# The first four token tiles: centred before the transpose, scaled at the eviction

## Chip, cores and metric

The kernel runs on one core of a Trainium2 chip. A core has five engines that run side by side and meet only at semaphores: TensorE (PE; its weight loads are shown as PEld), VectorE (DVE), ScalarE (ACT), GpSimd (POOL) and SyncE (SP), which here issues every DMA. The metric is the device time of one execution in microseconds (us), median of the runs. All matrix operands are bf16, all sums f32.

## What is computed

There are 2048 tokens of width 512, and four layers that alternate two blocks A, B, A, B with the same weights: `x = x + A(layernorm(x))`, then `x = x + B(layernorm(x))`. The layer norm has no gain and no bias. Block B is `relu(x @ w1) @ w2` with an inner width of 1376. Block A is linear attention with 32 heads of width 16:

```
q, k, v = split(x @ wqkv)                 # each 2048 x 512
phi(t) = where(t > 0, t + 1, exp(t)) + 1e-6
kv  = sum over tokens of phi(k) v^T       # 16 x 16 for each head
z   = sum over tokens of phi(k)
o   = (phi(q) @ kv) / (phi(q) . z + 1e-6)
out = o @ wo
```

## The kernel before

**Tiles.** The tokens are 16 tiles of 128, or 4 chunks of 4 tiles. In SBUF `xin` holds the input, `xres` the f32 residual, `xn` the normalised rows, `Tb` their transposes, `big` the results of the projections. PSUM has 8 banks of 128x512 f32.

**Who sets the order.** Every operation is recorded with a name, its engine, what it reads and writes and an assumed cost. `_list_schedule` then makes one fixed order for each engine from those costs. `HINTS` shifts the rank of single operations, and `SEQS` fixes the first operations of an engine. On the chip every engine runs its list strictly in that order and waits on semaphores where the data demand it. Because one helper issues all matrix products, the profile gives them one line, L558; the names below are those of the recorded operations, with the layer or tile number at the end.

**Layer 0, where the change lies.** SP first issues the loads: tile 0 of x, tiles 1 to 3, the K part of `wqkv` in two halves (`ld_wk0`, `ld_wk1`), the next x chunk, the Q part (`ld_wq`), the other x chunks, the V part, `wo`, and then `w1` and `w2` for block B (L413 to L417). Meanwhile PE runs 11 matrix products on zeros (`warm`).

For tiles 0 to 2 DVE computes mean and variance (`bnst`, `bnag`) and adds epsilon (`veps_`), POOL raises that to the power -1/2 (`rstd_`), and DVE writes the normalised row to `xn` (`norm`, L814). ACT makes the sums for tile 3. PE then transposes a tile as four 128x128 blocks (`trp`, L523), and ACT or DVE copies the result from PSUM to `Tb` (`trev`, L527 and L528). Tiles 4 to 7 go the same way, with 1/sqrt by a logarithm and an exponential on ACT (`lnv`, `rstd`, L463 and L465). Tiles 8 to 15 are transposed by DMA (`tr2_0`, `tr2_1`, `tr3_0`, L506).

The K projection (`kproj`, four products of 512 columns) takes a tile of `Tb` as the stationary side, so that its result has tokens on the partitions. The Q projection (`qproj t_j`) takes a 128-column piece of the weights as the stationary side and four tiles of `Tb` as the moving one, so that its result has features on the partitions. `phi_evac` turns each projection into phi: ACT writes t + 1 + 1e-6 (`_lin`, L541) and exp(t) (`_exp`, L543) from PSUM, DVE clips the exponential (`_em`, L545) and takes the maximum of both (`_phi`, L551). A PSUM bank is free again when both have read it.

The products `g` (phi(k) with `xn`, for sum phi(k) x^T) are spread among the projections. `den` makes the denominators, 1/den is spread over partitions by 16 DMAs (`spread`), DVE multiplies it into phi(q) (`pqs`), and `fin` gives the output of block A, which DVE adds to x (`resid`).

Of the kernel before, what the change touches and what calls it, by code (L numbers as in the profile page):

```python
# [47 lines left out]
HINTS = {"0.fin8_0": -99, "0.g0_1_3": 10, "0.g1_1_1": 30, "0.g1_2_1": -496, "0.g1_2_2": -77, "0.k4_em": -180, "0.k5_em": -110,  # L48
         "0.pqs3_3": 37, "0.q0_0_em": 80, "0.q0_2_em": -70, "0.q0_2_phi": 30, "0.q0_3_em": 33, "0.q3_2_lin": 177, "0.q3_3_lin":
         30, "0.resid8": -373, "0.spread1_3": -17, "2.fin13_0": 200, "2.g0_0_0": 80, "2.norm0": -160, "2.q3_3_lin": 3,  # L50
         "2.qproj3_1": 10, "2.qproj3_2": -80, "2.spread0_0": 3, "2.spread0_3": -230, "2.spread1_0": 30, "2.spread1_2": 57,
         "2.var1": 610, "3.ffo10": 284, "3.h3_3_0": 83}

SEQS = {
    "dve": ["bnst0", "bnag0", "veps_0", "bnst1", "bnag1", "norm0", "veps_1", "bnst2", "trev0b", "bnag2", "veps_2", "norm1", "norm3",
            "norm2", "trev2"],
    "act": ["mean_3", "sq_3", "trev0a", "lnv_3", "rstd_3", "trev1", "trev3", "k0_lin", "k0_exp"],
    "pool": ["rstd_0", "nm2_3", "var_3", "veps_3", "rstd_1", "rstd_2"],
    "pe": ["trp0a", "trp0b", "kproj0a", "trp1", "kproj0b", "trp3", "kproj1", "trp2", "kproj3", "qproj0_0", "kproj2"],
}  # L60

# [208 lines left out]
def build_kernel(nc, A_x, A_wqkv, A_wo, B_w1, B_w2, out, n_layers_pairs=2, K_STT=0, Q_STT=0, A_PE_CHUNKS=0, windows=None,  # L270
                 WARM=11, SPLIT0=True, TAIL_SPLIT=True, LAST_HALVES=True, FIRST_PE_CHUNKS=2,
# [13 lines left out]
    EPS = 1e-5  # L285
# [5 lines left out]
    with es:  # L291
# [4 lines left out]
        xres = sb("xres", [128, NT, 512], F32)  # L296
        wqkv = sb("wqkv", [128, 4, 3 * D], BF16)
# [20 lines left out]
        NSCR = 12  # L318
        escr = sb("escr", [128, NSCR, 512], BF16)
# [86 lines left out]
        for t in range(2, NCH):  # L406
            ld_x(t)
        dma(lambda e: e.dma_start(wqkv[:, :, 2 * D:3 * D], wq_v[:, :, 2 * D:3 * D]), [], [("wv0",)], 1500.0, "ld_wv")
        dma(lambda e: e.dma_start(wvl[:], A_wqkv[D - 1:D, 2 * D:3 * D].broadcast_to([128, D])), [], [("wvl",)], 400.0, "ld_wvl")
        dma(lambda e: e.dma_start(wo[:], A_wo.rearrange("(c p) n -> p c n", p=128)), [], [("wo",)], 1500.0, "ld_wo")  # L410
        nfull = NFC - 1 if FLAST < 128 else NFC

        dma(lambda e: e.dma_start(w1[:], B_w1.rearrange("(c p) n -> p c n", p=128)), [], [("w1",)], 4000.0, "ld_w1")  # L413
        dma(lambda e: e.dma_start(w2[:, 0:nfull, :], B_w2[0:nfull * 128, :].rearrange("(c p) n -> p c n", p=128)),
            [], [("w2a",)], 3800.0, "ld_w2a")
        if FLAST < 128:
            dma(lambda e: e.dma_start(w2[0:FLAST, NFC - 1, :], B_w2[nfull * 128:DFF, :]), [], [("w2b",)], 600.0, "ld_w2b")  # L417
# [8 lines left out]
        if WARM > 0:  # L426
            wt = alloc_bank()

            def _warm(e):
                last = None  # L430
                for k in range(WARM):
                    last = e.matmul(psv[:, wt, :], wrm[:, 0:128], wrm[:, :], start=True, stop=True)
                return last
            g.add(PE, _warm, [("wrm",)], [("ps", wt)], 10 * 427.0 + (WARM - 10) * 216.0, name="warm")
# [23 lines left out]
        def ln_part_first(lo, hi):  # L458
            sl = slice(lo, hi)
            tl = range(lo, hi)  # L460
            g.add(DVE, lambda e: e.tensor_scalar(veps[:, sl], mv[:, sl, 1], 0.0, EPS, ALU.max, ALU.add),
                  [("var", i) for i in tl], [("veps1", i) for i in tl], C_DVE_SMALL, name="veps%d" % lo)
            g.add(ACT, lambda e: e.activation(var[:, sl], veps[:, sl], ACTF.Ln), [("veps1", i) for i in tl], [("lnv", lo)],  # L463
                  C_ACT_TINY, name="lnv%d" % lo)
            g.add(ACT, lambda e: e.activation(rstd[:, sl], var[:, sl], ACTF.Exp, scale=-0.5), [("lnv", lo)],  # L465
                  [("rstd", i) for i in tl], C_ACT_TINY, name="rstd%d" % lo)
# [70 lines left out]
        def phi_evac(b, dst_ap, dst_key, name, stt):  # L537
            s = scr_state["e"]
            scr_state["e"] = (s + 1) % NSCR
            if not stt:  # L540
                g.add(ACT, lambda e: e.activation(dst_ap, psv[:, b, :], ACTF.Identity, bias=1.0 + 1e-6, scale=1.0),  # L541
                      [("ps", b)], [dst_key], C_ACT_PSUM, name=name + "_lin")
            g.add(ACT, lambda e: e.activation(escr[:, s, :], psv[:, b, :], ACTF.Exp),  # L543
                  [("ps", b)], [("escr", s)], C_ACT_EXP, name=name + "_exp")
            g.add(DVE, lambda e: e.tensor_scalar(escr[:, s, :], escr[:, s, :], 1.0, 1e-6, ALU.min, ALU.add),  # L545
                  [("escr", s)], [("escr", s)], C_DVE_BF4X, name=name + "_em")
            if stt:
                g.add(DVE, lambda e: e.scalar_tensor_tensor(dst_ap, psv[:, b, :], 1.0 + 1e-6, escr[:, s, :], ALU.add, ALU.max),
                      [("ps", b), ("escr", s)], [dst_key], C_DVE_PSUM, name=name + "_phi")
            else:  # L550
                g.add(DVE, lambda e: e.tensor_tensor(dst_ap, dst_ap, escr[:, s, :], ALU.max),  # L551
                      [dst_key, ("escr", s)], [dst_key], 340.0, name=name + "_phi")
# [25 lines left out]
        def a_k(i):  # L578
# [5 lines left out]
            phi_evac(b, pk_tile(i), ("big", pk_unit(i)), "k%d" % i, stt=(i % 4) < K_STT)  # L584
# [64 lines left out]
        def a_q(t, js=(0, 1, 2, 3)):  # L649
            for j in js:  # L650
# [5 lines left out]
                phi_evac(b, unit_ap(u), ("big", u), "q%d_%d" % (t, j), stt=j < Q_STT)  # L656

        def a_den(t):
# [3 lines left out]
            mm_group(lambda: [(psv[32 * j:32 * j + 32, b, :], Zc[:, j, :], unit_ap(pq_unit(j, t)), True, True, False) for j in range(4)],  # L662
                     [("Zc",)] + [("big", pq_unit(j, t)) for j in range(4)], [("ps", b)], 400.0, "den%d" % t)
# [15 lines left out]
        def a_pqs(t):  # L679
            for j in range(4):  # L680
                u, r = pq_unit(j, t), rb_unit(t, j)
                g.add(DVE, lambda e, u=u, r=r: e.tensor_tensor(unit_ap(u), unit_ap(u), unit_ap(r), ALU.mult),
                      [("big", r), ("big", u)], [("big", u)], 340.0, name="pqs%d_%d" % (t, j))

        def a_fin_mm(i, b, js):
            t, il = i // 4, i % 4

            def mk():
                mms = []
                for j in js:  # L690
                    u = pq_unit(j, t)
                    mms.append((psv[:, b, :], big[:, u * 512 + 128 * il:u * 512 + 128 * il + 128], Mf[:, j, :], j == 0, j == 3, False))
                return mms
            mm_group(mk, [("big", pq_unit(j, t)) for j in js] + [("Mf", j) for j in js], [("ps", b)],
# [109 lines left out]
        def ln_own(i):  # L804
            mu = mv[:, i, 0:1] if i < 3 else mean[:, i:i + 1]
            if i == 3:
                g.add(ACT, lambda e: e.activation(var[:, i:i + 1], veps[:, i:i + 1], ACTF.Ln), [("veps1", i)], [("lnv1", i)],
                      C_ACT_TINY, name="lnv_%d" % i)
                g.add(ACT, lambda e: e.activation(rstd[:, i:i + 1], var[:, i:i + 1], ACTF.Exp, scale=-0.5), [("lnv1", i)],
                      [("rstd1", i)], C_ACT_TINY, name="rstd_%d" % i)  # L810
            else:
                g.add(POOL, lambda e: e.tensor_tensor(rstd[:, i:i + 1], veps[:, i:i + 1], nhalf[:, 0:1], ALU.pow),
                      [("veps1", i), ("nhalf",)], [("rstd1", i)], C_POOL_POW1, name="rstd_%d" % i)
            g.add(DVE, lambda e: e.tensor_scalar(xn[:, i, :], xin[:, i, :], mu, rstd[:, i:i + 1], ALU.subtract, ALU.mult),  # L814
                  [("xin", i), ("mean", i), ("rstd1", i)], [("xn", i)], C_DVE_NORM_BF, name="norm%d" % i)
            transpose_pe(i)

        def ln_first(t):
            if t == 0 and SPLIT0:
                for i in range(3):  # L820
                    ln_stats_first(i, [[], [("veps1", 0)], [("xn", 0), ("veps1", 1)]][i])
                    g.add(DVE, lambda e, i=i: e.tensor_scalar(veps[:, i:i + 1], mv[:, i, 1:2], 0.0, EPS, ALU.max, ALU.add),  # L822
                          [("var", i)], [("veps1", i)], C_DVE_TINY, name="veps_%d" % i)
                    ln_own(i)
# [8 lines left out]
                g.add(POOL, lambda e: e.tensor_scalar(veps[:, 3:4], var[:, 3:4], 0.0, EPS, ALU.max, ALU.add),  # L833
                      [("var", 3)], [("veps1", 3)], 150.0, name="veps_3")
                ln_own(3)
                ones_col(0)
# [272 lines left out]
```

## Time and profile before

| | |
|---|---|
| device time, median of 3 runs | 281.34 us (281.33 to 281.36) |
| span of the profiled execution, first to last instruction | 279.2 us |
| so outside that span | about 2.1 us |
| PE busy | 274.7 us, 98% |
| ACT busy | 174.4 us, 62% |
| DVE busy | 139.3 us, 50% |
| POOL busy | 43.4 us, 16% |
| granted TensorE clock | 1.000 |

The page gives one time of the profiled execution itself, its span. The times of the three runs are taken from outside and are 2.1 us longer; that part lies before the first and after the last instruction. Busy time of PE is not a measure of its speed, because the ends of its products are modelled; what tells whether PE lost time is the distance from start to start. Shares over the whole span hide the beginning, where the change lies: the windows and the timeline of the first 30 us have to be read for it.

### The profile page before, as it was taken

The numbers are of one execution on the slowest core, as the hardware profiler recorded it, in microseconds if no ns is written. First come the engines' busy times: TensorE is split into PE (matmuls) and PEld (weight loads), VectorE is DVE, ScalarE is ACT, GpSimd is POOL, SyncE is SP. The second block draws the span as 40 slices with busy tenths as digits, with TensorE's granted clock in tenths as the row PEclk, the third lists the DMA queues.
The fourth block names the chain that finished last, engine by engine and source line by source line (L and its number), as shares of the span: only waits on it lengthen the run. The fifth ranks groups of instructions, "written<-read, shape, count | busy, mean of one in ns | idle before, by whom it ended". The sixth has DMA issues, their size and how long they took to land.

```text
span 279.2 us, 4216 instructions
## 1 busy us (share of the span) xinstructions
PE 274.7 (98%) x1574; PEld 140.2 (50%) x1574; DVE 139.3 (50%) x379; ACT 174.4 (62%) x367; POOL 43.4 (16%) x120
## 2 busy tenths in 40 slices
PE   7999999999999999999999999999999999999996
PEld 2546556546544544544444455664654554454443
DVE  5999963899301362443363576279935300110222
ACT  5899978778773682677373799765884376226000
POOL 6000000046300160400040400003136100000000
PEclk9999999999999999999999999999999999999999
DMA  6999300833900053060003030084331641021012
GB/s 215 367 378 160 58 2 17 199 87 76 171 19 0 2 96 75 0 96 0 0 10 68 0 75 0 2 191 115 75 77 20 167 77 21 0 75 21 0 75 75
DMA packets 44276, 22.09 MB, mean 79 GB/s; under 512 B 34560, under 2 KB 42720, under 8 KB 44256
## 3 DMA queue, kind: packets, MB, share of 16 engines
q1 hardware_dynamic: 44256, 21.83, 32.9%
q8 instruction: 12, 0.20, 0.3%
q14 instruction: 8, 0.07, 0.1%
HBM read 7.14 MB, written 2.10 MB: 33 GB/s over the span
## 4 chain that ended last, share of the span: by engine, by line
PE 97%; DVE 1%; DMA 1%; issue 0%; DVEq 0%
PE ps L558 96%; DMA xin<-in_A_x_dram 1%; DVE bst L455 1%; PE ps L523 1%; DVE xn L814 0%; DVE mv L456 0%; DVE veps L822 0%; DVE xin L774 0%; DVE Tb L528 0%; DVEq L1037 0%
## 5 line engine op out<-in xcount | busy, mean ns | idle before, releaser
L558 PE MATMUL ps<-w,big 128*128 128x512 bf16 (+3 forms) x363 | 77.5, 373 | 0.0
L558 PE MATMUL ps<-Tb,w 128*128 128x512 bf16 (+1 forms) x352 | 70.9, 360 | 0.0
L754 ACT ACTIVATE big<-ps 128x512 bf16<-128x512 f32 x72 | 42.8, 596 | 24.7 <-PE ps L558 24.6
L558 PEld LDWEIGHTS ps<-w,big 128*128 128x128 bf16 (+1 forms) x363 | 35.0, 98 | 41.2 <-ACT big L754 0.3
L558 PEld LDWEIGHTS ps<-Tb,w 128*128 128x128 bf16 x352 | 33.9, 98 | 32.8
L575 ACT ACTIVATE sqscr<-xres 128x512 bf16<-128x512 f32 x48 | 29.9, 623 | 30.0 <-DVE xres L569 29.7
L541 ACT ACTIVATE big<-ps 128x512 bf16<-128x512 f32 x64 | 41.1, 646 | 6.0 <-PE ps L558 6.0
L569 DVE SCALAR_TENSOR_TENSOR xres<-ps,xres 128x512 f32<-128x512 f32 x32 | 21.2, 689 | 43.4 <-PE ps L558 43.4
L543 ACT ACTIVATE escr<-ps 128x512 bf16<-128x512 f32 x64 | 41.4, 655 | 1.3 <-PE ps L558 1.3
L566 DVE TENSOR_TENSOR xin<-ps,xres 128x512 bf16<-128x512 f32 x15 | 10.4, 691 | 49.7 <-PE ps L558 49.7
L558 PE MATMUL ps<-big,xn 128*128 128x256 bf16 (+1 forms) x224 | 31.0, 288 | 0.0
L558 PE MATMUL ps<-Tb,wqkv 128*128 128x512 bf16 x128 | 30.6, 379 | 0.0
L558 PE MATMUL ps<-wqkv,Tb 128*128 128x512 bf16 x128 | 30.1, 379 | 0.4 <-ACT Tb L527 0.4
L558 PE MATMUL ps<-Mf,big 128*128 128x512 bf16 x128 | 28.8, 379 | 0.0
L545 DVE TENSOR_SCALAR escr<-escr 128x512 bf16<-128x512 bf16 x64 | 18.3, 293 | 20.2 <-ACT escr L543 19.9
L551 DVE TENSOR_TENSOR big<-big,escr 128x512 bf16<-128x512 bf16 x64 | 26.5, 425 | 1.4
L558 PEld LDWEIGHTS ps<-big,xn 128*128 128x128 bf16 x224 | 21.5, 98 | 9.0 <-issue 0.8
L471 POOL TENSOR_SCALAR mean<-s 128x4 f32<-128x4 f32 x12 | 2.9, 245 | 123.9 <-DVE xres L569 123.9
L558 PEld LDWEIGHTS ps<-Mf,big 128*128 128x128 bf16 x128 | 12.3, 98 | 14.6 <-ACT Mf L645 0.5
L558 PEld LDWEIGHTS ps<-wqkv,Tb 128*128 128x128 bf16 x128 | 12.2, 98 | 14.3 <-ACT Tb L527 0.7
L558 PEld LDWEIGHTS ps<-Tb,wqkv 128*128 128x128 bf16 x128 | 12.4, 98 | 12.7 <-DVE Tb L528 0.3
L493 DVE TENSOR_SCALAR xn<-xres,mean,rstd 128x512 bf16<-128x512 f32 x23 | 14.8, 679 | 3.7 <-POOL nbias L483 3.5
(78 smaller groups left out, 188.2 us busy)
## 6 DMA issues: line engine op xcount, KB each, us to landing
big<-rdc SPq DMA_DIRECT2D x32, 128.0 KB, 2.6
xin<-in_A_x_dram SPq DMA_DIRECT2D x3, 512.0 KB, 7.2
w<-in_B_w_dram SPq DMA_DIRECT2D x1, 1376.0 KB, 13.7
w<-in_B_w_dram SPq DMA_DIRECT2D x1, 1280.0 KB, 15.0
wqkv<-in_A_wqkv_dram SPq DMA_DIRECT2D x2, 512.0 KB, 7.4
out_dram<-xin SPq DMA_DIRECT2D x2, 512.0 KB, 2.7
wqkv<-in_A_wqkv_dram SPq DMA_DIRECT2D x2, 256.0 KB, 4.5
wo<-in_A_wo_dram SPq DMA_DIRECT2D x1, 512.0 KB, 10.6
```

Of the source, the lines that this page charges most:

```text
L455: g.add(DVE, lambda e: e.bn_stats(bst[:, i, :], xin[:, i, :]), [("xin", i)] + list(after), [("bst", i)], C_DVE_BNST, name="bnst%d" % i)
L471: g.add(POOL, lambda e: e.tensor_scalar(mean[:, sl], s1[:, sl], -INV_D, None, ALU.mult), [("s1", i) for i in tl], [("mean", i) for i in tl ...
L493: ts = (POOL, lambda e: e.tensor_scalar(xn[:, i, :], src, mean[:, i:i + 1], rstd[:, i:i + 1], ALU.add, ALU.mult), C_POOL_NORM)
L541: g.add(ACT, lambda e: e.activation(dst_ap, psv[:, b, :], ACTF.Identity, bias=1.0 + 1e-6, scale=1.0), [("ps", b)], [dst_key], C_ACT_PSUM, ...
L543: g.add(ACT, lambda e: e.activation(escr[:, s, :], psv[:, b, :], ACTF.Exp), [("ps", b)], [("escr", s)], C_ACT_EXP, name=name + "_exp")
L545: g.add(DVE, lambda e: e.tensor_scalar(escr[:, s, :], escr[:, s, :], 1.0, 1e-6, ALU.min, ALU.add), [("escr", s)], [("escr", s)], C_DVE_BF4 ...
L551: g.add(DVE, lambda e: e.tensor_tensor(dst_ap, dst_ap, escr[:, s, :], ALU.max), [dst_key, ("escr", s)], [dst_key], 340.0, name=name + "_phi")
L558: last = e.matmul(o, l, r, start=st, stop=sp, skip_group_check=skip)
L566: g.add(DVE, lambda e: e.tensor_tensor(xin[:, i, :], psv[:, b, :], src, ALU.add), [("ps", b), skey], [("xin", i)], C_DVE_PSUM, name="resid ...
L569: g.add(DVE, lambda e: e.scalar_tensor_tensor(xres[:, i, :], psv[:, b, :], 0.0, src, ALU.add, ALU.add, accum_out=s1[:, i:i + 1]), [("ps", ...
L575: g.add(ACT, lambda e: e.activation(sqscr[:, q, :], xres[:, i, :], ACTF.Square, accum_out=s2[:, i:i + 1]), [("xres", i)], [("sqscr", q), ( ...
L754: g.add_flex([(ACT, lambda e, M=M, b=b, u=u: e.activation(unit_ap(u, M), psv[0:M, b, :], ACTF.Relu), C_ACT_PSUM), (DVE, lambda e, M=M, b=b ...
```

## The change

1. **Tiles 0 to 3 are transposed without rstd.** `norm` on DVE is replaced by `center` (x minus mean), and PE transposes that. The rstd of a token is applied when its projection leaves PSUM, as the per-partition `scale` of the two ACT activations. POOL writes the full normalised row to `xn` later (`xn_first`), for the `g` products.
2. **The Q projection of these tiles gets tokens on the partitions** (`qtok`), so that the scale can be applied there. Four DMA transposes (`trq`, from SP) turn phi(q) into the form that the rest wants, in the memory of the last two tiles of `xres` (`pqf`). `den0`, `pqs0` and `fin0` to `fin3` read it there.
3. **Norm statistics on POOL.** `veps` goes from DVE to POOL for all 16 tiles, and `lnv` and `rstd` from ACT to one POOL power.
4. **`w1` and `w2` are issued later**, behind the DMA transposes of tiles 8 to 15.
5. **Twelve more buffers for the exponentials** of layer 0, in `xres`.
6. For `k6`, `k7` and `q3_3` (`STT`) the linear part is left out on ACT; DVE adds and takes the maximum from PSUM in one instruction.
7. 8 warm-up products instead of 11; new `HINTS` and `SEQS` for layer 0, so that the order of all engines there is a new one. The order of layers 1 to 3 stays nearly as it was.

The core of the diff:

```diff
-                 WARM=11, SPLIT0=True, TAIL_SPLIT=True, LAST_HALVES=True, FIRST_PE_CHUNKS=2,
+                 WARM=8, SPLIT0=True, TAIL_SPLIT=True, LAST_HALVES=True, FIRST_PE_CHUNKS=2,
...
+STT = {"0.k6", "0.k7", "0.q3_3"}
...
+        pqf = xres[:, NT - 2:NT, :].rearrange("p i d -> p (i d)").bitcast(BF16).rearrange("p (i j k) -> p i j k", j=4, k=128)
...
-        dma(lambda e: e.dma_start(w1[:], B_w1.rearrange("(c p) n -> p c n", p=128)), [], [("w1",)], 4000.0, "ld_w1")
-        dma(lambda e: e.dma_start(w2[:, 0:nfull, :], B_w2[0:nfull * 128, :].rearrange("(c p) n -> p c n", p=128)),
-            [], [("w2a",)], 3800.0, "ld_w2a")
...
         def ln_part_first(lo, hi):
-            g.add(DVE, lambda e: e.tensor_scalar(veps[:, sl], mv[:, sl, 1], 0.0, EPS, ALU.max, ALU.add),
-            g.add(ACT, lambda e: e.activation(var[:, sl], veps[:, sl], ACTF.Ln), [("veps1", i) for i in tl], [("lnv", lo)],
-            g.add(ACT, lambda e: e.activation(rstd[:, sl], var[:, sl], ACTF.Exp, scale=-0.5), [("lnv", lo)],
+            g.add(POOL, lambda e: e.tensor_scalar(veps[:, sl], mv[:, sl, 1], 0.0, EPS, ALU.max, ALU.add),
+            g.add(POOL, lambda e: e.tensor_tensor(rstd[:, sl], veps[:, sl], nhalf[:, 0:hi - lo], ALU.pow),
...
         def phi_evac(b, dst_ap, dst_key, name, tok=None):
+            sc = 1.0 if tok is None else rstd[:, tok:tok + 1]
             if not stt:
+                g.add(ACT, lambda e: e.activation(dst_ap, psv[:, b, :], ACTF.Identity, bias=1.0 + 1e-6, scale=sc),
+            g.add(ACT, lambda e: e.activation(esc, psv[:, b, :], ACTF.Exp, scale=sc),
...
+        def a_q_tok():
+            for i in FIRST_ORDER:
+                b = alloc_bank()
+                mm_group(lambda b=b, i=i: [(psv[:, b, :], Tb[:, i, c, :], wqkv[:, c, 0:D], c == 0, c == 3, False) for c in range(4)],
+                         [("T", i), ("wq",)] + ([("T0a", 0)] if i == 0 else []), [("ps", b)], 4 * C_MM512, "qtok%d" % i)
+                u = pq_unit(i, 0)
+                phi_evac(b, unit_ap(u), ("big", u), "q0_%d" % i, tok=i)
+                dma(lambda e, i=i, u=u: e.dma_start_transpose(pqf[:, i, :, :], unit_ap(u)),
+                    [("big", u)] + list(ALL_LOADS), [("pqf", j, i) for j in range(4)], 700.0, "trq%d" % i, issue=1300.0)
...
+        def center(i, mu):
+            g.add(DVE, lambda e: e.tensor_scalar(xn[:, i, :], xin[:, i, :], mu, None, ALU.subtract),
+                  [("xin", i), ("mean", i)], [("xn", i)], C_DVE_NORM_BF, name="cent%d" % i)
+            transpose_pe(i)
...
+        FIRST_ORDER = (0, 3, 1, 2)
+        def xn_first():
+            for i in FIRST_ORDER:
+                mu = mv[:, i, 0:1] if i < 3 else mean[:, i:i + 1]
+                g.add(POOL, lambda e, i=i, mu=mu: e.tensor_scalar(xn[:, i, :], xin[:, i, :], mu, rstd[:, i:i + 1], ALU.subtract, ALU.mult),
```

The new orders of the engines, as far as the prediction needs them, each in the sequence in which the engine runs them:

```
PE    warm trp0 trp3 kproj0a trp1 kproj0b kproj3 trp2 kproj1 kproj2 qtok3 qtok0 qtok1 trp4 trp5 qtok2 kproj4
      trp6 trp7 kproj5 kproj6 qproj1_2 qproj1_0 kproj7 qproj1_3 qproj1_1 g0_3_0 .. g0_2_0 kproj8 9 10 11 ...
      qproj3_1 g0_3_3 .. g0_2_3 zcol g1_0_0 den0 den2 ...
DVE   ... cent2 trev2 bnst4 bnst5 bnag4 k3_em bnag5 k3_phi bnst6 bnst7 bnag6 norm4 bnag7 norm5 k1_em bnst8 trev4
      norm6 norm7 bnst11 .. bnag10 k0_em k1_phi k0_phi k5_em bnst14 norm8 .. norm11 ... k7_phi q1_0_phi k6_em
      q1_2_em k6_phi norm12 ...
POOL  veps_0 nm2_3 veps_1 rstd_1 var_3 rstd_0 veps_3 rstd_3 veps_2 norm3 veps4 rstd4 rstd_2 veps6 rstd6
      norm0 norm1 onec1 norm2 veps8 onec0 rstd8 ...
SP    loads up to wo, tr2_0 tr2_1 tr3_0 ld_w1 ld_w2a ld_w2b trq1 trq0 trq3 trq2 spread0 spread2 spread1 spread3
```

`kproj11` takes the PSUM bank that `k6_phi` gives back, and `trp6` and `trp7` wait for `norm6` and `norm7`.

## The prediction

> **What bounds the kernel now.** I read the page's busy times and slices first, then the chain of waits, then the timeline of the first 30 us.
>
> ```profile
> PE 274.7 (98%) x1574; PEld 140.2 (50%) x1574; DVE 139.3 (50%) x379; ACT 174.4 (62%) x367; POOL 43.4 (16%) x120
> ...
> DVE  5999963899301362443363576279935300110222
> ...
> 15.56 261.11 PE ps L558 x1499
> ```
>
> PE is the bound. The chain shows more: from 15.56 us to the end it is one piece of PE, 261 us without a wait. No edit can gain anything there; it can only put waits in. What can be gained lies before 15.4 us. The slices (7 us each) show DVE full from 7 to 35 us, so DVE is the engine that stands next to the bound just where the change works.
>
> ```profile
> 1.24 4.14 PE L432 MATMUL ps<-wrm 128*128 128x512 bf16 x11 [1.24 <-DVE wrm L425]
> ...
> 6.18 0.60 PE L558 MATMUL ps<-wqkv,Tb 128*128 128x512 bf16 x2 [0.36 <-ACT Tb L527]
> ...
> 7.06 0.40 PE L523 MATMUL ps<-ident,xn 128*128 128x128 bf16 x4 [0.27 <-DVE xn L814]
> ...
> 15.39 3.62 PE L558 MATMUL ps<-wqkv,Tb 128*128 128x512 bf16 x16
> ```
>
> The timeline of the start gives the work and its price: in unbroken stretches a 512-column product takes 0.216 us from start to start (16 in 15.39 to 18.85), a 256-column one 0.109, a tile of four transposes 0.22. From 6.18 to 15.39 (9.21 us) lie 32 products and 7 tiles, 6.91 + 1.54 = 8.45 us of work. So 0.76 us were lost, most of it waiting for normalised rows.
>
> **The start on PE.** Centred rows need no rstd, so the transposes of tiles 0 and 3 move up to about 4.7 and 5.3 us. The first projection doesn't: it also needs the weights.
>
> ```profile
> L402 SPq DMA_DIRECT2D wqkv<-in_A_wqkv_dram x2: 426/448/470, 1.7 to 2.2; - x2
> ...
> DMA to landing us min/median/max: 4.3/4.5/4.7
> ```
>
> The two K halves were issued at 1.72 and 2.18 us, so they landed at about 6.05 and 6.84, and SP's order up to there is unchanged. `kproj0a` can start at 6.10 instead of 6.18: 0.08 us gained, not the 0.8 that the transposes gain. `kproj0b` waits for the second half: 6.10 + 0.43 + 0.22 (`trp1`) = 6.75, against 6.89, a new wait of 0.14. The transposes of tile 3 (0.22) now lie before 6.10, in dead time, and the 0.76 of losses go, since `trp1` and `trp2` wait for centring alone. Gain: 0.08 + 0.76 + 0.22 - 0.14 = **0.92 us**, if nothing new holds PE. The token-major Q is 16 products of 512 columns as before, and `ld_wq` (landed 9.6) is not reached before 10.1. The three warm-up products that go ended before the 5.42 of the old first transposes: nothing.
>
> **DVE, next in line.** Its list up to `k6_phi`, whose bank `kproj11` takes, is from the timeline's distances: 12 `bnst` at 0.59, 12 `bnag` at 0.09, 11 `em` at 0.20, 8 `phi` at 0.34, 8 `norm` at 0.32, `trev4` 0.32, and two PSUM instructions of 0.61 and 0.69 (`k7_phi`, `k6_phi`; priced by the residual adds, 689 ns): 17.26 us. It begins later than before: `trev2` stands ahead of `bnst4` and waits for `trp2`, behind `kproj3` on PE, 8.57 us; so `bnst4` starts at 8.93 instead of 8.19. The same prices over the old list, from 8.19 to the old `k6_phi`, give 24.21 where the timeline has 24.05, so I take 0.16 off: `k6_phi` ends at 26.03, and `kproj11` may start at 26.08. PE without a stall gets there at 6.10 + 0.14 + 76 x 0.216 + 6 x 0.22 + 2.17 (`g`) = 26.15. The slack is 0.07 us: from here on what DVE loses, PE loses.
>
> ```profile
> 8.20:27.00 18.80, 18.80 (x114) 10.16 (x115) 18.80 (x65) 18.50 (x44) 0.37 (x3) 1.00 1.04 306
> ```
>
> In that window (PE, PEld, DVE, ACT, POOL) DVE was busy for all of 18.80 us and POOL for 0.37. The change puts four normalisations and nearly all statistics on POOL there. What such neighbours do to each other later layers show:
>
> ```profile
> L493 DVE TENSOR_SCALAR xn<-xres,mean,rstd x23: 527/545/994, 62.0 to 217.5; 128x512 bf16<-128x512 f32 x23
> ...
> 71.06 0.77 POOL L493 TENSOR_SCALAR xn<-xres,mean,rstd 128x512 bf16<-128x512 f32 x1
> 71.11 0.99 DVE L493 TENSOR_SCALAR xn<-xres,mean,rstd 128x512 bf16<-128x512 f32 x1 [1.31 <-POOL nbias L483]
> ...
> 117.92 1.09 POOL L493 TENSOR_SCALAR xn<-xres,mean,rstd 128x512 bf16<-128x512 f32 x1
> 118.00 1.29 DVE L493 TENSOR_SCALAR xn<-xres,mean,rstd 128x512 bf16<-128x512 f32 x2
> ```
>
> A DVE normalisation takes 0.53 us alone and 0.99 when POOL's began 0.05 us before it: 0.46 lost. Where DVE came first, POOL took 1.09 instead of 0.77, and the second of the DVE pair still lost 0.30. `norm6` waits for `rstd6`, and POOL runs `norm0` straight behind `rstd6`, so this meeting is certain; `trev4` makes `norm6` 0.15 late anyway, so it costs 0.3. `norm1` (about 14.6 us) meets `norm7`: 0 to 0.46, and I take 0.46, since in all seven cases where the two began within 0.1 us of each other DVE lost 0.3 or more. `norm3` runs beside copies from PSUM and `bnst`, `norm2` beside `bnst`; I take 0, with 0.46 as the other end. POOL's small steps also wait for DVE (the power took 1.32 at most against 1.03), which delays `rstd4`, `norm4`, `trp4`: 0 to 0.3, taken as 0.1. Sum 0.86, less the slack 0.07: **0.8 us** of PE waits, at `trp5`, `trp7` and `kproj11`. Bounds: none (the bf16 rows might not meet) to 4 x 0.46 + 0.3 = 2.1.
>
> The Trainium skill, page "SBUF — State Buffer", section "SBUF: two separate sides", calls this pair of ports an exclusive lock that the first holds for its whole instruction. By that rule a meeting would cost the whole 0.77 and not 0.46, and with my two meetings the sum would be 281.8 instead of 281.2, towards rival (b). The rows have DVE finish 0.27 us after POOL with 0.53 us of its own work, so the lock ended sooner than the rule says, and I stay with 0.46.
>
> **ACT.** 16 activations get a pointer scale. The normalisations on ACT have two pointers and take 814 ns, the squares over the same f32 rows 629: 0.09 a pointer, 1.5 us in all. Off ACT go ten short instructions (0.10 to 0.25) and two PSUM reads at 0.48 by 25 us, about 2.2 us. In between, before `trev6`, 12 scaled ones cost 1.1 and only 0.7 is off; `kproj5` waits for `trev6`. I take 0; ends 0 and 0.3.
>
> **SP and the DMAs.** `w1` and `w2` are wanted only from about 67 us (`hr0`), and moved in 7.3 us before. Issued behind `tr3_0` (issue about 27.6, landing 4.25 later by its old row) they end near 39. The four `trq` queue behind them. A transpose of that size took 1.26 us to issue and 2.8 to land, so the last lands near 41.5 to 42.5; `den0` needs all four at about 43.6 (it was at 44.68, and has 0.9 us less in front of it). Nothing, by 1 to 2 us. `spread`, behind them on SP, waits for `den0` anyway. `tr2_0` lands 3.3 us after its issue near 20.2, just when `kproj8` is reached: 0, at most 0.4.
>
> **Sum.** 281.34 - 0.92 + 0.8 = **281.2 us**. I add to the median of the runs, since span and outside (279.2 and 2.1) change alike.
>
> **Rivals.**
> (a) POOL and DVE don't meet in a way that counts, and the 0.92 is kept up to the 0.14 by which DVE or ACT may be late: 280.56. For it: `bnst` and PSUM copies fill much of DVE's list, and they showed no stretch. Against it: `norm6` and `norm0` are released together.
> (b) Slower: DVE is the bound. If all four normalisations and the small steps cost it 2.1 us, and ACT's 0.3 comes on top: 281.34 - 0.92 + 2.1 + 0.3 = 282.8. It decides from a loss of 1.5 us on. For it: 18.80 of 18.80.
> (c) `den0` waits for `trq2`. This row speaks for it:
>
> ```profile
> 10.55 7.34 SPq L417 DMA_DIRECT2D w<-in_B_w_dram  x1
> ```
>
> SP was held 7.3 us issuing the last piece of `w2`. Held as long from 31 us on, the four issues end at 43.4, landing at 46: 2.4 us later than wanted, 283.6. Against it: before, 6.6 us of other loads stood ahead, now none.
> (d) The clock. The warm-up's weight loads are 0.43 us apart until 4.20 and then two within 0.31 at 4.57, so full speed came 3.3 us after the first product; eight products end at 4.66, 0.1 later. If it came later, up to 3.4 us would run at half speed: 283.0. The Trainium skill, "TensorE: Matmul & The Clock Gate", Part 1, says the same of a free-running window of about 3.4 us that must be busy; no run here shows its phase.
>
> **Chances.** Forecast, within 0.2% (0.56 us, about what can be told from no change): 0.44. (a) 0.27. (b) 0.19. (c) 0.07. (d) 0.03. So faster 0.27, same 0.44, slower 0.29. Range 280.4 to 282.7: it holds the forecast, (a), and most of (b); the forecast's own range is 280.8 to 281.8.
>
> **What would show it.** `kproj0a` at 6.1 us and `kproj0b` waiting for the weights; short PE waits for `xn` near 13 and 15 us and for a bank near 26; the DVE normalisations L487 near 14 us at 0.7 us or more instead of 0.4; POOL's near 0.8 or more; no wait ahead of `den0`. The prediction is wrong if PE is unbroken from 7 us on (a), or breaks also at `g0_3_0`, `kproj5` or `den0` (b, c), or if the products after 4.7 us are 0.43 apart (d).

## The result, and the profile after

The changed kernel takes **285.98 us** (285.76 to 287.41), the kernel before 281.36 us beside it: a ratio of 1.0166 (95% interval 1.0145 to 1.0187), so it is slower by 4.6 us. The forecast was 281.2 us, no change, with a range of 280.4 to 282.7. The profiled execution has a span of 284.0 us, 4.8 more than before.

Three lines of the page of the changed kernel: the busy times, and the slices (7.1 us each) of DVE and POOL.

```profile
PE 274.1 (96%) x1551; PEld 140.0 (49%) x1571; DVE 139.4 (49%) x371; ACT 174.5 (61%) x355; POOL 58.1 (20%) x136
...
DVE  5869992589800253271444387469943500020223
...
POOL 6891100013800071130040300002334200000000
```

PE is as busy as before in a longer span: the time went into its waits. DVE, full from 7 to 35 us before, now has a hole in its third slice, the one in which POOL is full. The list of what PE waited for (us in total, times, longest), without the beginning:

```profile
PE ps L566 <- DVE mv L456: 2.6, 1, 2.6
...
PE ps L566 <- DMA xres<-big: 1.3, 1, 1.3
PE ps L566 <- DMA Tb<-xn: 0.5, 1, 0.5
PE ps L566 <- DVE big L556: 0.3, 1, 0.3
```

All four are new: in the kernel before, that list has no wait after 7.1 us. The first is put down to `mv`, but of the 16 products of that group one has no record; the weight loads show what it was. Each wait has its place.

**At 24.6 us, `g0_3_0`.** The timeline of the changed kernel from 16.4 to 24.7 us (start, duration, engine, line; in brackets the idle time ahead and its releaser):

```profile
16.44 2.08 POOL L893 TENSOR_SCALAR xn<-xin,mv,rstd 128x512 bf16<-128x512 bf16 x1
...
18.55 2.11 POOL L893 TENSOR_SCALAR xn<-xin,mv,rstd 128x512 bf16<-128x512 bf16 x1
...
20.64 0.26 POOL L461 TENSOR_SCALAR veps<-mv 128x4 f32<-128x4 f32 x1
...
20.92 0.69 DVE L455 BATCH_NORM_STATS2 bst<-xin 128x6 f32<-128x512 bf16 x1 [2.21 <-POOL veps L461]
...
20.98 1.04 POOL L463 TENSOR_TENSOR rstd<-veps,nhalf 128x4 f32<-128x4 f32 x1
...
22.05 1.38 DVE L487 TENSOR_SCALAR xn<-xin,mv,rstd 128x512 bf16<-128x512 bf16 x4 [0.43 <-POOL rstd L463]
...
24.15 0.41 DVE L559 TENSOR_TENSOR big<-big,escr 128x512 bf16<-128x512 bf16 x1
...
24.61 1.09 PEld L566 LDWEIGHTS ps<-big,xn 128*128 128x128 bf16 x7 [2.90 <-DVE big L559]
```

Read it backwards. PE's weight load waits 2.9 us for `k2_phi` (L559). That stands on DVE behind `norm8` to `norm11` (L487), which wait for `rstd8` (L463) on POOL. DVE has nothing to do ahead of them either, since `bnst14` (L455) waits 2.2 us for `veps8` (L461). `rstd8` and `veps8` stand behind `norm1` and `norm2` (L893), though the statistics that they need were there 3 us before: POOL is simply not done. A normalisation there takes 2.1 us, where the prediction had 0.77.

**At 29.8 us, `kproj11`.** It waits for `k6_phi` (L556), which the same delay on DVE has pushed back: 0.3 us, and 0.8 on the weight load.

**At 47.9 us, `den0`.** The timeline of the changed kernel, SP's issues and PE's line at `den0`:

```profile
22.81 10.00 SPq L504 DMA_TRANSPOSE Tb<-xn  x3
32.85 1.19 SPq L898 DMA_DIRECT2D w<-in_B_w_dram  x1
34.09 0.52 SPq L899 DMA_DIRECT2D w<-in_B_w_dram  x1
34.65 2.57 SPq L902 DMA_DIRECT2D w<-in_B_w_dram  x1
37.27 7.22 SPq L674 DMA_TRANSPOSE xres<-big  x4
...
47.88 0.40 PE L566 MATMUL ps<-xres,Zc 128*32 128x512 bf16 x4 [1.33 <-DMA xres<-big]
```

and, from the view of line L674 there, the time from issue to landing of the four `trq`:

```profile
DMA to landing us min/median/max: 4.6/5.9/7.7
```

The whole queue starts 2.6 us later than the 20.2 us of the prediction, because `tr2_0` waits for `norm8` and `norm9`, which end at 22.79 us. Then each `trq` takes 1.3 to 2.5 us to issue and 4.6 to 7.7 to land.

**At 206.4 us, in front of the last layer.** The same timeline there, two transposes on SP and PE's wait for the second:

```profile
200.91 3.30 SPq L504 DMA_TRANSPOSE Tb<-xn  x2
...
206.40 0.51 PE L566 MATMUL ps<-w,Tb 128*128 128x96 bf16 x8 [0.51 <-DMA Tb<-xn]
```

The same two in the kernel before:

```profile
196.33 2.61 SPq L506 DMA_TRANSPOSE Tb<-xn  x2
```

There the second issue follows 0.12 us behind the first and PE does not wait; in the changed kernel 0.53 us lie between them. The change edits nothing there.

### The profile page after: what moved, and what is told of

It is laid out like the page before. It is cut to its first block, busy times and chain, and to the rows that moved or that the text cites. A ratio compares the mean times of both kernels' runs of the same rounds, so it can differ in the third digit from the quotient of the medians.

```text
span 284.0 us, 4191 instructions
## 1 busy us (share of the span) xinstructions
PE 274.1 (96%) x1551; PEld 140.0 (49%) x1571; DVE 139.4 (49%) x371; ACT 174.5 (61%) x355; POOL 58.1 (20%) x136
## 4 chain that ended last, share of the span: by engine, by line
PE 79%; DVE 6%; POOL 4%; DMA 4%; ACT 4%; issue 1%; SPq 0%; POOLq 0%
PE ps L566 79%; POOL xn L893 2%; ACT big L548 2%; DMA xres<-big 2%; DVE bst L455 2%; DVE xres L577 1%; DMA Tb<-xn 1%; DMA xin<-in_A_x_dram 1%; ACT escr L550 1%; DVE big L559 1%; ACT xres L550 1%; POOL rstd L463 1%; DVE xn L487 0%; POOL rstd L479 0%; DVE escr L552 0%
## 5 line engine op out<-in xcount | busy, mean ns | idle before, releaser
L793 ACT ACTIVATE big<-ps 128x512 bf16<-128x512 f32 x71 | 42.3, 597 | 24.6 <-PE ps L566 24.5
L583 ACT ACTIVATE sqscr<-xres 128x512 bf16<-128x512 f32 x48 | 29.9, 623 | 29.8 <-DVE xres L577 29.5
L548 ACT ACTIVATE big<-ps 128x512 bf16<-128x512 f32 x53 | 33.2, 630 | 6.7 <-PE ps L566 6.7
L566 PE MATMUL ps<-wqkv,Tb 128*128 128x512 bf16 x138 | 32.9, 379 | 0.7 <-DVE big L556 0.3
L550 ACT ACTIVATE escr<-ps 128x512 bf16<-128x512 f32 x44 | 28.2, 640 | 1.0 <-PE ps L566 1.0
L566 PE MATMUL ps<-Tb,wqkv 128*128 128x512 bf16 x112 | 26.3, 379 | 0.0
L552 DVE TENSOR_SCALAR escr<-escr 128x512 bf16<-128x512 bf16 x52 | 15.3, 297 | 20.4 <-ACT escr L550 20.2
L566 PE MATMUL ps<-Mf,big 128*128 128x512 bf16 x109 | 24.7, 379 | 0.2
L566 PEld LDWEIGHTS ps<-wqkv,Tb 128*128 128x128 bf16 x144 | 13.7, 98 | 16.7 <-DVE big L556 1.0
L559 DVE TENSOR_TENSOR big<-big,escr 128x512 bf16<-128x512 bf16 x49 | 20.4, 423 | 1.1
L496 ACT ACTIVATE xn<-xres,nbias,rstd 128x512 bf16<-128x512 f32 x15 | 11.9, 815 | 9.2 <-POOL nbias L481 9.2
L566 PEld LDWEIGHTS ps<-Mf,big 128*128 128x128 bf16 x112 | 10.9, 98 | 13.0 <-ACT Mf L654 0.2
```

What stands on the lines that cost most here:

```text
L496: (ACT, lambda e: e.activation(xn[:, i, :], src, ACTF.Identity, scale=rstd[:, i:i + 1], bias=nbias[:, i:i + 1]), C_ACT_SB_AP)],
L550: g.add(ACT, lambda e: e.activation(esc, psv[:, b, :], ACTF.Exp, scale=sc), [("ps", b)] + rk, [ekey], C_ACT_EXP + xd, name=name + "_exp")
L552: g.add(DVE, lambda e: e.tensor_scalar(esc, esc, 1.0, 1e-6, ALU.min, ALU.add), [ekey], [ekey], C_DVE_BF4X, name=name + "_em")
L559: g.add(DVE, lambda e: e.tensor_tensor(dst_ap, dst_ap, esc, ALU.max), [dst_key, ekey], [dst_key], 340.0, name=name + "_phi")
L566: last = e.matmul(o, l, r, start=st, stop=sp, skip_group_check=skip)
L583: g.add(ACT, lambda e: e.activation(sqscr[:, q, :], xres[:, i, :], ACTF.Square, accum_out=s2[:, i:i + 1]), [("xres", i)], [("sqscr", q), ( ...
```

## The experiments

The executions differ at the start: `kproj5` begins at 15.5 to 18.3 us in the changed kernels, among other things since the loads land at different times (`wk1` at 6.05 to 7.82 us in these traces). So beside the timed ratio I give the **rest**: the profiled span less the start of `kproj5`'s first weight load. Up to `kproj5` all changed kernels have done the same work, in the same order on PE. The rest of the changed kernel is 284.0 - 15.95 = 268.05 us. Each rest comes from one profiled execution; the changed kernel's two differ by 0.2 us.

### What a normalisation on GpSimd costs

> The kernel before with extra instructions behind its last addition, so that its time grows by their sum (some 30 to 45 us); the output is the same. GpSimd alone first: two normalisations from the f32 residual, two from the bf16 input, then one-operation, constant-operand and 256-wide forms; then two of each source beside a row of VectorE instructions. Theory T (the type of the source sets GpSimd's price): bf16 source 2.1 us with no neighbour at all, f32 source 0.77 us; VectorE's 128x512 bf16 tensor_scalar stays at about 0.33 us beside the bf16 ones and is stretched by up to 0.46 us beside the f32 ones. Rival N (the neighbour sets it: the 2.1 us are waiting for VectorE): bf16 source 0.77 to 0.85 us alone, and 2 us only beside VectorE's row.

The kernel before, with this behind its last addition:

```diff
...
+            for src, kw in ((f32, {}), (f32, {}), (b16, {}), (b16, {}), (b16, dict(two=False)), (f32, dict(two=False)),
+                            (b16, dict(ptr=False)), (b16, dict(w=256)), (f32, dict(w=256))):
+                last = ts(POOL, xn[:, 0, :], src, "p", reads=last, **kw)
...
```

`ts` subtracts and multiplies, or with `two=False` multiplies alone.

The timeline of POOL in that run, behind the end of all other work:

```profile
278.14 4.27 POOL L997 TENSOR_SCALAR xn<-xres,mean,rstd 128x512 bf16<-128x512 f32 x2 [59.77 <-DVE xin L774]
282.51 4.24 POOL L997 TENSOR_SCALAR xn<-xin,mean,rstd 128x512 bf16<-128x512 bf16 x2
286.85 1.57 POOL L998 TENSOR_SCALAR xn<-xin,rstd 128x512 bf16<-128x512 bf16 x1
```

and the later layers' normalisations in the same trace (times in ns, min/median/max):

```profile
L493 POOL TENSOR_SCALAR xn<-xres,mean,rstd x10: 762/767/1091, 68.6 to 217.6; 128x512 bf16<-128x512 f32 x10
```

Both theories fall, by the instructions of this one execution. There is no neighbour, so N is out; and the f32 source costs 2.1 us as well, so the type is out. Even a single multiplication takes 1.57 us, twice the 0.77 us of L493. The difference that is left between L493 and these, besides the place in the program, is the operation: `add` and `mult` there, `subtract` and `mult` here.

> The kernel before with extra GpSimd and VectorE instructions behind its last addition; the output is the same. The first such run had the f32 source at 2.07 to 2.10 us too, so the type of the source is out. In order: add/mult from f32, add/mult from bf16, subtract/mult from f32, subtract/mult from bf16, mult/add from bf16, add alone, subtract alone, add/mult with constants, add/mult again; then four add/mult of each source beside sixteen VectorE normalisations of 0.41 us. Theory O (the pair of operations sets GpSimd's price): add/mult 0.77 us from either source, subtract/mult 2.07 to 2.10 us from either. Rival W (the place: GpSimd is slower wherever the residual layers' own lines are not running): add/mult costs 2.1 us here as well. Contention: if the prediction's 0.46 us for a meeting holds, each add/mult stretches one VectorE instruction by 0.41 to 0.46 us, as each of the 2.1 us ones stretched one to two.

```diff
...
+            for src, a, o0, b, o1 in ((f32, m, A, r, M), (b16, m, A, r, M), (f32, m, S, r, M), (b16, m, S, r, M), (b16, r, M, m, A),
+                                      (b16, m, A, None, None), (b16, m, S, None, None), (b16, 0.5, A, 0.25, M), (b16, m, A, r, M)):
+                last = ts(POOL, src, a, o0, b, o1, reads=last)
...
```

`A`, `S` and `M` are add, subtract and mult; `m` and `r` are columns of the mean and of rstd.

POOL's timeline again, in the order of that list:

```profile
277.88 0.77 POOL L999 TENSOR_SCALAR xn<-xres,mean,rstd 128x512 bf16<-128x512 f32 x1 [59.75 <-DVE xin L774]
278.75 0.77 POOL L999 TENSOR_SCALAR xn<-xin,mean,rstd 128x512 bf16<-128x512 bf16 x1
279.62 2.10 POOL L999 TENSOR_SCALAR xn<-xres,mean,rstd 128x512 bf16<-128x512 f32 x1
281.82 2.08 POOL L999 TENSOR_SCALAR xn<-xin,mean,rstd 128x512 bf16<-128x512 bf16 x1
284.00 0.77 POOL L999 TENSOR_SCALAR xn<-xin,rstd,mean 128x512 bf16<-128x512 bf16 x1
284.87 3.25 POOL L999 TENSOR_SCALAR xn<-xin,mean 128x512 bf16<-128x512 bf16 x2
288.21 0.62 POOL L999 TENSOR_SCALAR xn<-xin 128x512 bf16<-128x512 bf16 x1
```

and the VectorE instructions beside the first four `add`/`mult` that follow (ns):

```profile
L999 DVE TENSOR_SCALAR xn<-xin,mean,rstd x5: 415/833/834, 289.7 to 292.6; 128x512 bf16<-128x512 bf16 x5
```

Theory O holds. `add`/`mult` and `mult`/`add` take 0.77 us from either source, `subtract`/`mult` 2.1 from either; `add` or `subtract` alone takes 1.6. Beside each of the four 0.77 us instructions one VectorE instruction was stretched, the first from 0.41 to 0.67 us and the other three to 0.83: 0.42 for a meeting, against the 0.46 of the prediction. Beside each of 2.1 us in the run before, two VectorE normalisations were stretched, by 0.25 to 0.42 us each and 0.7 to 0.8 together; those between them passed at their usual 0.41. The Trainium skill, "SBUF — State Buffer", section "SBUF: two separate sides", has the first hold the ports for its whole instruction. By that, VectorE would stand still for 2.1 us each time; the trace doesn't agree.

> The changed kernel, with GpSimd's four bf16 normalisations cut to the first 188 of 512 columns (the rest of these rows stays without rstd, so the output differs): at 2.1 us for 512 columns that makes them 0.77 us, the price of the prediction. Every order stays. Theory T (their length, and rstd8 queued behind them, costs the wait at the group g0_3_0 and part of those at kproj10 and kproj11): 285.98 - 2.6 - 0.6 = 282.8 us (282.3 to 283.3), PE's wait at g0_3_0 under 0.5 us, and den0 still waiting for trq2 by 1 to 1.6 us. Rival N (what costs is that GpSimd works beside VectorE): half the beside-time goes, 284.5 to 285.5. If the prediction's other terms were all right: 281.2, with no wait at den0.

```diff
-                g.add(POOL, lambda e, i=i, mu=mu: e.tensor_scalar(xn[:, i, :], xin[:, i, :], mu, rstd[:, i:i + 1], ALU.subtract, ALU.mult),
+                g.add(POOL, lambda e, i=i, mu=mu: e.tensor_scalar(xn[:, i, 0:188], xin[:, i, 0:188], mu, rstd[:, i:i + 1], ALU.subtract, ALU.mult),
```

282.92 us against 281.76: 1.0043 (1.0022 to 1.0064), as theory T had it. The rest is 264.7 us, 3.3 less than in the changed kernel. The instructions took 1.0 us, not 0.77. PE waits no longer at `g0_3_0` and `kproj11`, and still 1.0 us at `den0` and 0.5 in front of the last layer.

> The changed kernel with its four GpSimd normalisations written as add of the negated mean and mult by rstd instead of subtract and mult, as the later layers have them; the negated means cost one GpSimd instruction on 128x3 (0.25 us) and a changed sign in ScalarE's mean of tile 3. All orders stay. Theory O: each takes 0.77 us, or 1.1 us beside VectorE, rstd8 ends near 18.2 instead of 22.0 us, the wait at g0_3_0 goes, den0 still waits 1.0 us for trq2 and the late transposes 0.5 us: like the run with the norms cut to 188 columns, 1.003 to 1.005 of the kernel before (282.3 to 282.9 us). Rival W (not the operation): 2.1 us each, 1.015 to 1.018, 285.6 to 286.4 us.

```diff
...
-                g.add(POOL, lambda e, i=i, mu=mu: e.tensor_scalar(xn[:, i, :], xin[:, i, :], mu, rstd[:, i:i + 1], ALU.subtract, ALU.mult),
+                mu = mean[:, i:i + 1]
+                g.add(POOL, lambda e, i=i, mu=mu: e.tensor_scalar(xn[:, i, :], xin[:, i, :], mu, rstd[:, i:i + 1], ALU.add, ALU.mult),
...
+        neg = _Op(POOL, lambda e: e.tensor_scalar(mean[:, 0:3], mv[:, 0:3, 0], -1.0, None, ALU.mult), (), (), 250.0, 0.0, False, "nneg")
...
```

The row of the normalisations in that run:

```profile
L894 POOL TENSOR_SCALAR xn<-xin,mean,rstd x4: 767/770/934, 9.3 to 18.8; 128x512 bf16<-128x512 bf16 x4
```

283.26 us, 1.0082 (1.0038 to 1.0126): about half of what the change had lost is back, from one word and a sign. By its median that is less than the 1.003 to 1.005 expected, though the interval reaches into it. The runs lie far apart (282.1 to 285.5), and the profiled one, the slowest, began late: `kproj5` at 18.27 us. Tiles 1 to 3 of x landed at 5.29 instead of 4.31 us, which is 1.0 us. The other 1.3 us goes with the speed of PE. Of the two lines that follow, the first is from the changed kernel, the second from this run, each the same six products:

```profile
6.72 1.47 PE L566 MATMUL ps<-wqkv,Tb 128*128 128x512 bf16 x6
...
8.16 2.64 PE L566 MATMUL ps<-wqkv,Tb 128*128 128x512 bf16 x6
```

Until 10.6 us the products here start 0.43 us apart, as in the warm-up, instead of 0.216. The rest, 265.5, which leaves all that out, is 2.5 below the changed kernel's. The wait at `g0_3_0` is gone.

### Its place in GpSimd's list

> The changed kernel with one thing moved: on GpSimd veps8 and rstd8 stand in front of norm2 instead of behind it. Theory T: rstd8 ends at 20.1 instead of 22.0 us, norm8 to norm11 and k2_phi come 1.8 us earlier, g0_3_0 then waits for onec0 (22.5) and k2_phi (22.4) alone: 1.6 to 1.9 us less, 284.2 us (284.0 to 284.7). Rival N (contention with VectorE): the normalisation meets the same VectorE work, 285.6 to 286.2. Rival Q (the transfers at den0 set the end whatever comes before): the gain at g0_3_0 is given back at den0, 285.5 to 286.

```diff
-            "veps6", "rstd6", "norm0", "norm1", "norm2"],
+            "veps6", "rstd6", "norm0", "norm1", "veps8", "rstd8", "norm2"],
```

285.07 us, 1.0115 (1.0088 to 1.0142). The rest is 266.9 us, 1.2 less, where 1.6 to 1.9 was expected. The timeline of that run shows where the other part stayed:

```profile
20.73 2.09 POOL L893 TENSOR_SCALAR xn<-xin,mv,rstd 128x512 bf16<-128x512 bf16 x1
...
20.77 2.19 DVE L487 TENSOR_SCALAR xn<-xin,mv,rstd 128x512 bf16<-128x512 bf16 x4 [0.43 <-POOL rstd L463]
```

Counted from `kproj5`, `rstd8` came 2.1 us sooner. But `norm2` on POOL now runs beside `norm8` to `norm11`, and these take 2.19 us instead of 1.38: 0.8 us lost to the meeting, as much as a 2.1 us instruction cost VectorE above. So PE's wait at `g0_3_0` fell only from 2.6 to 1.2 us, and a new one of 0.7 us came at `kproj8`, for `tr2_0`, while the 0.3 at `kproj11` went. The time lies 0.3 us above theory T's range and below the rivals', while the kernel before took 0.4 us more here than in the first comparison. So theory T comes nearest, but does not have it whole: the queue behind the long instruction costs, and where that instruction meets VectorE, that costs as well.

### The weight loads in front of the transposed Q

> The changed kernel with one thing moved: the three issues of w1 and w2 stand behind the four trq on SP's queue instead of in front of them; every other order stays. Theory S (trq2 is late because it is issued behind the three weight loads and shares the engines with them): trq1 is issued near 33 us instead of 37.3, the last trq lands by 41, den0 runs when zc is ready at about 46.3, and the run takes 285.98 - 1.5 = 284.5 us (284.1 to 284.9); the wait at g0_3_0 stays at 2.6. Rival D (den0 is held by Zc or the first spread anyway): 285.7 to 286.1. Rival W (w1 and w2 then meet the spreads from 48 us on and hold them): 286 to 288, with VectorE's products pqs waiting for the spread tile.

```diff
+        ws = [o for o in order[SP] if o.name in ("ld_w1", "ld_w2a", "ld_w2b")]
+        rest = [o for o in order[SP] if o not in ws]
+        k = max(j for j, o in enumerate(rest) if o.name.startswith("trq")) + 1
...
+        order[SP][:] = rest[:k] + ws + rest[k:]
```

The four `trq` in that run, issue on SP and landing:

```profile
L674 SPq DMA_TRANSPOSE xres<-big x4: 1265/1270/1915, 33.7 to 38.2; - x4
...
DMA to landing us min/median/max: 2.5/2.5/3.1
```

284.69 us, 1.0115 (1.0068 to 1.0163); the rest is 266.4, 1.65 less, as theory S had it. Without the weights in flight a `trq` lands after 2.5 us instead of 5.9, the last at 40.8 us, and PE doesn't wait for it, nor for a spread behind the later weights. The wait at `g0_3_0` stays, at 2.4 us, and here, where all 16 products have a record, it is put down to `k2_phi` itself.

> The same with the three issues of w1 and w2 behind the four trq on SP's queue. Theory S (den0's wait is the weight loads' place) with theory O: another 1.0 us less, 1.000 to 1.001 of the kernel before (281.3 to 281.8 us); no wait on the transposed Q. If den0 has another releaser just behind trq2: 1.002 to 1.004. Neither theory gives a gain over the kernel before above 0.2%, since the start's lead of 1.3 us at 12 us has shrunk to 0.3 us at 20 us in the changed kernel.

Both edits together: 282.38 us, 1.0034 (1.0011 to 1.0057), where 1.000 to 1.001 was expected. The rest is 264.2. No wait at `den0`, but 0.3 us at `kproj8` for `tr2_0`, and 0.6 in front of the last layer.

### The gap between two transposes at 200 us

> The run with add/mult and the weights behind the trq, with twenty further wait instructions (already met, and in a place where SP idles, in front of the first transfer of the second layer) on SP. In all changed kernels so far SP issues the second transpose into the fourth layer 0.53 us after the first (before: 0.12 us) and it lands 3.7 to 3.8 us later (before 3.1), so that PE waits 0.2 to 0.6 us at 3.hr0_1 and the last layer begins some 0.8 us later than it could. Theory I (that gap goes with the place of this instruction in SP's instruction stream, which the change has shifted): the gap at this transpose falls to about 0.1 us or moves to another instruction, 0.4 to 0.8 us less, 1.000 to 1.002 of the kernel before. Rival O (what the other engines do at that time, as planned, sets it): the gap stays at 0.5 us and the run at 1.003.

> The same with six waits instead of twenty. Theory I: the gap is again another one than with none or twenty (0.1 or 0.5 us, depending on where the stream's bounds fall). Rival O: 0.5 us, 1.003 of the kernel before.

```diff
...
+                if o.key == "1.trh0":
+                    for _ in range(6):
+                        handle.wait_ge(sem_eng[PE], 1)
...
```

(20 in place of 6 in the other.)

With six waits, the two transposes in SP's timeline,

```profile
196.48 2.62 SPq L504 DMA_TRANSPOSE Tb<-xn  x2
```

and that part of the chain that ended last, where PE now runs on without a wait from 190.59 to 209.82 us:

```profile
190.54 0.05 issue
190.59 19.23 PE ps L566 x117
```

With six waits 281.04 us against 281.69, a ratio of **0.9979** (0.9967 to 0.9990): faster than the kernel before, by 0.2%. With twenty 281.20, 0.9989 (0.9971 to 1.0006), which no difference would fit too. The rests are 263.05 and 263.1, 1.2 less than without: 0.8 of it in front of the last layer, where the gap fell from 0.53 to 0.10 us and PE's wait went. The other 0.4 lies at `kproj8`, where `tr2_0` landed sooner; SP's list up to there is the same with and without the waits, so I don't count that as their work.

> The changed kernel with nothing but the six extra wait instructions on SP. Theory I (place of SP's instructions): the 0.53 us gap between the two transposes into the fourth layer falls to 0.1 us, PE's 0.5 us wait there goes, and the run takes 0.6 to 0.9 us less than the changed kernel on this chip (285.5): 284.6 to 284.9, 1.010 to 1.012 of the kernel before; the waits at g0_3_0 and den0 stay. Rival O (the gap goes with the transposed Q's and the weights' order, which the padded runs also had changed): 285.2 to 285.7.

Here the timed runs do not decide: 285.22 us, 1.0142 (1.0108 to 1.0177), where 1.010 to 1.012 was expected. The trace shows more. The timeline of the changed kernel with the six waits, the same two places as above:

```profile
200.79 2.62 SPq L504 DMA_TRANSPOSE Tb<-xn  x2
...
205.62 0.50 PE L566 MATMUL ps<-w,Tb 128*128 128x96 bf16 x8
```

No gap and no wait; the rest is 267.1, 0.8 less than the 267.9 of the changed kernel's second profile, below.

> The kernel before with the same six waits. Its gap at this transpose is 0.12 us already, so theory I expects no gain: 0.999 to 1.001 if no bound of the stream moves into a place that matters, or a loss of 0.5 to 0.9 us if one does. If it were 0.998, the gain of the padded version over the kernel before would be the padding's and not that of the repaired change.

281.55 us, 1.000 (0.999 to 1.001). The gap came up here (the two transposes take 2.99 us on SP instead of 2.61) without a wait behind it. So the gain of the padded version isn't the padding's alone. Over all profiled executions the gap of 0.52 to 0.53 us stands in all seven of the changed kernels without added waits and in none of the three with them, and in the kernel before it is the other way round. That it goes with the place in SP's instruction stream is shown. The DMA packets say more. The view of the queues in the changed kernel, from 202.7 us (the second issue begins at 202.66) to 204.5:

```profile
q14 instruction: 1, 0.01, 2.3%
```

The view calls this a queue of instructions. In all eight profiles with the gap one 8 KB packet of it begins 0.63 to 0.66 us after the start of the second issue; in the six without the gap none begins within 2 us of that start. So the gap goes with a fetch of instructions, and instructions that are added move both. That the fetch is SP's own is likely, but the packets do not say whose they are. It begins after the gap, so SP did not wait for this packet; what fills the 0.5 us stays open.

> The changed kernel itself once more, on the chip of these runs, to set the others against: by the first comparison 1.0145 to 1.0187 of the kernel before; the profile with a wait of 2.4 to 2.9 us at g0_3_0 and of 1.2 to 1.6 us at den0.

285.49 us, 1.0137 (1.0122 to 1.0152), rest 267.9, with waits of 2.6 us at `g0_3_0`, 1.1 at `den0` and 0.5 in front of the last layer: the result again.

### What each piece is worth

| kernel | ratio to before | rest, us |
|---|---|---|
| changed | 1.0166 and 1.0137 | 268.05 and 267.9 |
| + add/mult | 1.0082 | 265.5 |
| + weights behind `trq` | 1.0034 | 264.2 |
| + six waits on SP | 0.9979 | 263.05 |

Each row has the edits of the rows above it too. The three steps take 2.5, 1.3 and 1.2 us off the rest, 5.0 together: more than the 4.6 that the change had cost. Of the 1.2 only 0.8 is the work of the six waits, as said above, and the one profile per row leaves each step uncertain by some 0.2 us.

## Why the prediction was wrong

**What bounds the kernel: right.** PE has no slack after the start, so every new wait showed in the time.

**Start on PE: right in size, near the forecast in effect.** `kproj0b` began at 6.72 us (forecast 6.75), `kproj0a` at 5.90 (6.10), since `wk0` landed at 5.33 instead of 6.05. Counting the products and transposes that had started, at 0.216 us for 512 columns, PE was about 1.2 us ahead of before at 12 us and 0.3 at 20 us: the start was gained, and most of it was lost again in waits for `norm` and `trev` on DVE, as the sum had it (0.92 less most of 0.8).

**DVE and its meetings: right in kind, too dear.** In the changed kernel `norm6` took 0.73 us instead of 0.40 and one `em` 0.55 instead of 0.26: 0.62 us lost, against the 0.86 of the sum. `norm7` met a POOL normalisation and lost nothing.

**The step that failed: POOL's normalisation at 0.77 us.** The price was taken from L493, as if a normalisation were one thing. L493 adds a negated mean, L893 subtracts the mean, and the trace of before had no row for that on POOL. So it was not a price but a guess without bounds of its own, and it carried "`norm2` beside `bnst`" at 0 and the silent assumption that `rstd8`, behind `norm2`, comes in time for `tr2_0`'s issue near 20.2 us. At 2.1 us each, `rstd8` came at 22.0: PE's 2.6 us at `g0_3_0`, the 0.3 at `kproj11`, and 2.6 us on the start of SP's queue. Cutting or repairing these four instructions alone took 3.3 or 2.5 us off the rest.

**The DMAs: rival (c), in smaller form and by another way.** The last weight piece held SP for 2.57 us, not for 7.3. But each `trq` was priced from rows without other traffic (1.26 us to issue, 2.8 to land) and took up to 2.5 and 7.7 with the weights in flight. Together with the late start of the queue that made 1.3 us at `den0` where 0 was taken.

**ACT's pointers: right.** The scaled activations take 0.68 to 0.70 us against 0.60 (one took 0.73), and PE waits for none.

**The clock: rival (d) was nearer than its chance of 0.03.** The granted clock of 1.000 tells nothing of the start: it reads 1.00 there even while the warm-up's products are 0.43 us apart. The prediction took the end of the slow time, 4.57 us, from one trace. In another profile of the kernel before (the one with six waits) the loads are 0.43 us apart up to 5.05 us, but eleven products cover that: in none of that kernel's four profiles is a product behind the warm-up slow. Of the ten profiles of changed kernels, five have slow ones, two products each in four of them and eight in the add/mult run. In the profile that the result was read from only the transposes of tile 0 and a part of tile 3 were slow, so this is no part of the losses there. Eleven warm-up products in the changed kernel were not tried.

Later the clock may have fallen too. Four of the changed kernel's five timed executions list 0.994, and so do six of twelve in the other runs with a wait of 2.4 to 2.6 us at `g0_3_0`; of the 46 executions of changed kernels without that wait none does. Their times are not longer by an amount that stands out: 285.23 and 285.68 us with 0.994, 285.42 and 285.56 with 1.000, in the changed kernel's second set. Where the clock fell, no trace shows.

**Not in the sum at all:** the 0.8 us in front of the last layer, from SP's shifted instructions.

With the three repairs the kernel is 0.3 us (twenty waits) or 0.6 us (six) faster than before; the forecast was 0.1, rival (a) 0.8. That this is the forecast's mechanism, the start's gain mostly eaten by DVE, fits but was not measured in that kernel.

## What to carry to other kernels

A price belongs to the exact instruction, with its operations, and not to what it computes: where the profile has no row of that form, bound it widely, or write it in a form that has one (on GpSimd add and mult instead of subtract and mult). When work moves to an idle engine, look at what stands behind it in that engine's list and who waits for that; the engine's free time says nothing of it. A warm-up cut to the length that one trace needed can run out in the next. And before a loss far from an edit is explained by the edit, see whether it survives a few instructions put in that do nothing.

## What the runs showed of the hardware

- GpSimd's `tensor_scalar` on 128x512 takes 0.77 us for add with mult, in either order, 1.56 to 1.59 us for one operation alone with a column operand, 2.07 to 2.10 us for subtract with mult; bf16 and f32 sources alike. One operation is dearer than the right two. The Trainium skill, "GPSIMD Engine Reference", section "3.1 Elementwise — side-by-side cycle accounting", gives a best case of about 1.8 cycles an element, 769 ns for 512: the add/mult rows agree, the others are far from it.
- A GpSimd instruction of 0.77 us stretched one VectorE instruction by 0.25 to 0.42 us; one of 2.1 us cost VectorE 0.7 to 0.8 in all.
- The same DMA transpose landed after 2.5 to 3.1 us without, and after 4.6 to 7.7 us with 2.8 MB of weights in flight.
- Six waits that were already met, on an idle queue, moved a 0.5 us gap between two issues that came over 120 us later. Each time the gap stood there, an 8 KB packet of the instruction queue began 0.63 to 0.66 us after the second issue.
- After eight warm-up products (0.43 us apart) the next ones ran at full speed (0.216 us) from the first in five of ten profiles, and in one not before 10.6 us.
